# Attention softmax denominators: reciprocals by GpSimd's power instruction, and all sums of exps made on VectorE

## The chip, the cores and the metric

One core of a Trainium2 chip. The metric is device microseconds of the whole kernel, the median of several executions. The engines are called as in the profile: PE (TensorE matmuls, PEld its weight loads), DVE (VectorE), ACT (ScalarE), POOL (GpSimd), SP (SyncE; all DMA issues on the page of before are its queue's, SPq).

## The reference, cut to what matters

A transformer block on 2048 tokens of width 1024: modulated layer norm, attention with 32 query heads of 32 that share one key and value head, output projection, then a second layer norm and a gated MLP of width 3584. The change touches one line of it, the softmax:

```python
scores = jnp.einsum('bhqd,bkd->bhqk', q, k) * Dh ** (-0.5)
p = _softmax(scores, axis=-1)
o = jnp.einsum('bhqk,bkd->bhqd', p, v)
```

## The kernel before

The kernel works on query blocks of 256, 256, 512, 512 and 512 tokens. Within a block it runs eight rounds, one for each group of four heads. In a round, PE makes scores (L704), ACT makes exps of them (L715) into a ring of ten buffers U, PE multiplies the exps by the values (L659) and adds the result to the numerators ASB, and the denominators of the four heads come to DSB. At the end of a round the product ASB/DSB is written over the queries in QT. While a block is in its rounds, PE fills its free time with the MLP of the block before. What is left runs after the last round, together with the last block's MLP; this is called the tail below.

The instructions are put in a fixed order by a list scheduler in the kernel's own code. It uses the durations that are written at each `G.add` as `dur`. Each engine gets its instructions in this fixed order.

The denominators come in one of two ways. For the first `NDIR` = 2 rounds of a block (0 in the first block), PE multiplies every exp tile by ones ("direct"). For the others DVE adds four exp tiles at a time (L744, L749) into a buffer TR, and PE multiplies these few sums by ones (L760):

```python
elif w == 1:
    G.add("dve", lambda e, tr=tr, u=u, fu=first_u: e.tensor_tensor(        # L744
        TR[:, tr, 0:4 * W], U[:, fu, 0:4 * W], U[:, u, 0:4 * W], ALU.add), ...)
else:
    G.add("dve", lambda e, tr=tr, u=u: e.tensor_tensor(                     # L749
        TR[:, tr, 0:4 * W], TR[:, tr, 0:4 * W], U[:, u, 0:4 * W], ALU.add), ...)
# ... (cut: dmm, the matmul by ones over the sums, into the PSUM bank of group g)
G.add("dve", lambda e, g=g: e.tensor_copy(DSB[:, 0:qn], PB[g.bank][:, 0:qn]), writes=["DSB"], ...)   # L766
for h in range(qn // 128):
    G.add("dve", lambda e, h=h: e.reciprocal(DSB[:, h * 128:(h + 1) * 128], DSB[:, h * 128:(h + 1) * 128]),
          reads=["DSB"], writes=[("DSBr", h), "DSB%d" % h], dur=0.87, ...)                            # L769
G.add("dve", lambda e, f=f: e.tensor_tensor(QT[:, f, q0:q0 + qn], ASB[:, 0:qn], DSB[:, 0:qn], ALU.mult),
      ..., writes=qkeys(f, q0, qn) + ["ATTD"], ...)                                                   # L771
```

There is one ASB and one DSB, and the matmuls by the values read the key "ATTD" that the product writes. So the first values batch of a round waits for the product of the round before, and an exp can only run ten buffers ahead of the values batches that free them.

The softmax here doesn't subtract the row's maximum and nothing guards it: scores larger than these inputs give would overflow.

## Time and profile before

| | before |
|---|---|
| time, median of the first 3 runs | 1299.66 us |
| profiled span | 1296.0 us |
| attention rounds, from 47 to 1097 us | 1050 us |
| tail, from 1097 us | 199 us |
| one steady round of 512 queries | 34.47 us |
| denominator's copy to product in such a round | 11.06 us |

The engine summary and the chain of waits, from the page of before. In the first line a figure is busy us, its share of the span in brackets and the number of instructions; in the others it is the share of the span that the chain spends on an engine or line:

```profile
PE 1177.5 (91%) x11393; PEld 583.5 (45%) x11393; DVE 877.7 (68%) x1223; ACT 1011.0 (78%) x1174; POOL 20.8 (2%) x51
...
PE 43%; ACT 41%; issue 6%; DVE 6%; DMA 3%; SPq 1%; ACTq 0%; DVEq 0%
```

Busy time by stretch in before: the length, then busy us and instructions of each engine, PE's clock and the DMA share.

```profile
47.00:1097.00 1050.00, 958.85 (x9773) 442.85 (x9766) 769.70 (x1022) 982.03 (x1131) 9.55 (x24) 0.97 0.34 95
1097.00:1296.00 199.00, 193.35 (x1285) 124.00 (x1283) 71.47 (x118) 16.72 (x28) 3.17 (x8) 1.00 0.47 132
```

The third busy figure is DVE's. In the rounds ACT is busy for 982 and PE for 959 of 1050 us, DVE for 770. So DVE, whose work the change moves, has the most room of the three.

Groups of instructions of before, from the page: line, engine, operation, output and input, count, then busy us and mean ns of one, then idle time of the engine just before them and what ended most of it:

```profile
L715 ACT ACTIVATE UREG<-SP 128x1024 bf16<-128x1024 f32 x1024 | 969.6, 1172 | 60.6 <-PE PB L659 32.1
...
L749 DVE TENSOR_TENSOR UREG<-UREG 128x2048 bf16<-128x2048 bf16 x200 | 243.2, 1216 | 31.8 <-ACT UREG L715 29.2
...
L744 DVE TENSOR_TENSOR UREG<-UREG 128x2048 bf16<-128x2048 bf16 x100 | 121.5, 1215 | 87.3 <-ACT UREG L715 86.7
...
L769 DVE RECIPROCAL DSB<-DSB 128x128 f32<-128x128 f32 x128 | 115.1, 927 | 0.5
```

And the only powers of before, the layer norms' inverse roots, from the POOL groups by shape:

```profile
L474 POOL TENSOR_TENSOR RS<-RS,NHALF 128x1 f32<-128x1 f32 x16 | 9.1, 571 | 1.3
L474 POOL TENSOR_TENSOR RS<-RS,NHALF 128x4 f32<-128x4 f32 x4 | 4.2, 1043 | 0.3
```

Finally the end of a steady round on DVE, from the timeline of before (start us, us, instruction), from the denominator's copy to the product 11.06 us later:

```profile
703.74 0.68 DVE L766 COPY DSB<-PB 128x512 f32<-128x512 f32 x1
...
714.80 0.68 DVE L771 TENSOR_TENSOR QT<-ASB,DSB 128x512 bf16<-128x512 f32 x1
```

### The profile page before, as it was taken

Reading aid. Unit: us, or ns where it says so; the run is one execution under the profiler, and the core shown is the slowest. Engines: PE = TensorE matmul, PEld = TensorE weight load, DVE = VectorE, ACT = ScalarE, POOL = GpSimd, SP = SyncE. Lnnn points to the kernel's source line nnn. Section 1 sums busy time; section 2 is a strip of 40 time slices with the busy share of each in tenths; the row PEclk is TensorE's granted clock in tenths of the full one; section 3 lists DMA queues with packets and bytes.
Section 4 is the critical chain, followed back from the end, with each engine's and each line's share of the span. In section 5 each row is a group of like instructions: output and inputs, shape, how many; then the busy total and the mean of one; then the engine's idle time right before and its main releaser. Section 6 shows DMA issues by size and latency. Waiting matters only on the chain.

```text
span 1296.0 us, 26693 instructions
## 1 busy us (share of the span) xinstructions
PE 1177.5 (91%) x11393; PEld 583.5 (45%) x11393; DVE 877.7 (68%) x1223; ACT 1011.0 (78%) x1174; POOL 20.8 (2%) x51
## 2 busy tenths in 40 slices
PE   5698998899898889868999999999999999999998
PEld 3343344554455555413333335545333336754477
DVE  7888867885457787746687777656887777633421
ACT  1499999999899999989999999989999996011100
POOL 1000000000000000000000000000000000000000
PEclk9898999999899999868999999999999999999999
DMA  9533001553456556500232344202433244255563
GB/s 313 195 103 112 2 2 50 148 155 107 114 133 176 144 151 181 145 1 2 66 89 84 90 121 112 62 1 67 130 98 94 83 109 115 60 174 150 161 173 90
DMA packets 239446, 141.31 MB, mean 109 GB/s; under 512 B 6880, under 2 KB 231136, under 8 KB 239328
## 3 DMA queue, kind: packets, MB, share of 16 engines
q1 hardware_dynamic: 239328, 139.61, 37.6%
q8 instruction: 90, 1.47, 0.5%
q14 instruction: 28, 0.23, 0.1%
HBM read 135.40 MB, written 4.19 MB: 108 GB/s over the span
## 4 chain that ended last, share of the span: by engine, by line
PE 43%; ACT 41%; issue 6%; DVE 6%; DMA 3%; SPq 1%; ACTq 0%; DVEq 0%
ACT UREG L715 38%; PE PB L809 9%; PE PB L838 7%; PE SP L704 5%; PE SP L809 5%; PE PB L659 5%; PE SP L838 5%; ACT HREG L818 3%; PE PB L786 2%; DMA WREG<-in_B_w_dram 1%; DVE UREG L744 1%; PE PB L554 1%; PE PB L760 1%; DMA WREG<-in_w_mod_dram 1%; DMA UREG<-in_w_mod_dram 1%
## 5 line engine op out<-in xcount | busy, mean ns | idle before, releaser
L715 ACT ACTIVATE UREG<-SP 128x1024 bf16<-128x1024 f32 x1024 | 969.6, 1172 | 60.6 <-PE PB L659 32.1
L809 PE MATMUL PB<-QT,WREG 128*128 128x512 bf16 (+1 forms) x1904 | 361.7, 331 | 6.8 <-DVE DSB L766 2.0
L749 DVE TENSOR_TENSOR UREG<-UREG 128x2048 bf16<-128x2048 bf16 x200 | 243.2, 1216 | 31.8 <-ACT UREG L715 29.2
L704 PE MATMUL SP<-QT,KT 32*128 32x512 bf16 (+1 forms) x2560 | 207.5, 348 | 57.8 <-ACT UREG L715 44.2
L809 PEld LDWEIGHTS PB<-QT,WREG 128*128 128x128 bf16 x1904 | 166.8, 98 | 160.7 <-issue 63.3
L744 DVE TENSOR_TENSOR UREG<-UREG 128x2048 bf16<-128x2048 bf16 x100 | 121.5, 1215 | 87.3 <-ACT UREG L715 86.7
L704 PEld LDWEIGHTS SP<-QT,KT 32*128 32x128 bf16 x2560 | 54.1, 92 | 245.4 <-ACT UREG L715 231.0
L838 PE MATMUL PB<-WREG,HREG 128*128 128x256 bf16 x1232 | 152.8, 273 | 2.7 <-DVE HREG L843 1.8
L659 PE MATMUL PB<-UREG,V 128*32 128x512 bf16 (+1 forms) x2528 | 138.1, 353 | 10.2 <-DVE HREG L820 4.6
L838 PEld LDWEIGHTS PB<-WREG,HREG 128*128 128x128 bf16 x1232 | 113.1, 98 | 40.3 <-issue 24.8
L818 ACT ACTIVATE HREG<-PB 128x512 bf16<-128x512 f32 (+1 forms) x126 | 82.2, 652 | 46.9 <-PE PB L809 42.7
L769 DVE RECIPROCAL DSB<-DSB 128x128 f32<-128x128 f32 x128 | 115.1, 927 | 0.5
L820 DVE SCALAR_TENSOR_TENSOR HREG<-HREG,PB 128x512 bf16<-128x512 bf16 (+1 forms) x126 | 71.0, 563 | 45.8 <-ACT HREG L818 37.7
L659 PEld LDWEIGHTS PB<-UREG,V 128*32 128x32 bf16 x2528 | 59.2, 99 | 69.9 <-issue 25.8
L818 ACT ACTIVATE HREG<-SP 128x512 bf16<-128x512 f32 x14 | 8.4, 597 | 94.5 <-PE SP L809 94.5
L809 PE MATMUL SP<-QT,WREG 128*128 128x512 bf16 x336 | 75.0, 379 | 0.0
L554 PE MATMUL PB<-HREG,WREG 128*128 128x512 bf16 x256 | 66.2, 384 | 1.2 <-DVE QT L557 1.1
L825 DVE TENSOR_TENSOR HREG<-HREG,PB 128x256 bf16<-128x256 bf16 (+1 forms) x112 | 60.8, 543 | 5.4 <-PE PB L809 3.9
L838 PE MATMUL SP<-WREG,HREG 128*128 128x256 bf16 x560 | 62.8, 273 | 1.3 <-DMA WREG<-in_B_w_dram 1.3
L838 PEld LDWEIGHTS SP<-WREG,HREG 128*128 128x128 bf16 x560 | 54.6, 98 | 8.8 <-DMA WREG<-in_B_w_dram 1.8
L786 PE MATMUL PB<-WO,QT 128*128 128x512 bf16 x208 | 54.7, 390 | 0.1
L809 PEld LDWEIGHTS SP<-QT,WREG 128*128 128x128 bf16 x336 | 32.9, 98 | 39.4
(88 smaller groups left out, 567.0 us busy)
## 6 DMA issues: line engine op xcount, KB each, us to landing
WREG<-in_B_w_dram SPq DMA_DIRECT2D x140, 512.0 KB, 4.1
WREG<-in_B_w_dram SPq DMA_DIRECT2D x20, 1792.0 KB, 8.2
X<-in_A_x_dram SPq DMA_DIRECT2D x32, 256.0 KB, 3.7
WREG<-in_w_mod_dram SPq DMA_DIRECT2D x16, 512.0 KB, 4.9
UREG<-in_w_mod_dram SPq DMA_DIRECT2D x8, 512.0 KB, 9.1
out_dram<-X SPq DMA_DIRECT2D x16, 256.0 KB, 3.4
WO<-in_A_wo_dram SPq DMA_DIRECT2D x1, 2048.0 KB, 16.0
WREG<-in_A_wq_dram SPq DMA_DIRECT2D x1, 1792.0 KB, 11.1
```

The source lines that it names most:

```text
L554: g = mm_group(NC, lambda e, b, c: e.matmul(b, WQ[:, c, f * P:(f + 1) * P], HT[:, c, sl], start=c == 0, stop=c == NC - 1), lambda c: [("WQ ...
L659: r = e.matmul(PB[g.bank][32 * gg:32 * gg + 32, 0:qn], V[:, kt, :] if kind == "V" else ONES[:], U[:, pu, (gg * npk + j) * qn:(gg * npk + j ...
L704: r = e.matmul(SP[:, b, o:o + w], KT[32 * gg:32 * gg + 32, kts[j] * P:(kts[j] + 1) * P], QT[32 * gg:32 * gg + 32, f, q0 + qo:q0 + qo + w], ...
L715: G.add("act", lambda e, u=u, h0=h0, n=n, b0=b0, nb=nb, wb=wb: e.activation(U[:, u, h0 * W:(h0 + n) * W].rearrange("p (b w) -> p b w", b=n ...
L744: G.add("dve", lambda e, tr=tr, u=u, fu=first_u: e.tensor_tensor(TR[:, tr, 0:4 * W], U[:, fu, 0:4 * W], U[:, u, 0:4 * W], ALU.add), reads= ...
L749: G.add("dve", lambda e, tr=tr, u=u: e.tensor_tensor(TR[:, tr, 0:4 * W], TR[:, tr, 0:4 * W], U[:, u, 0:4 * W], ALU.add), reads=[("TR", tr) ...
L769: G.add("dve", lambda e, h=h: e.reciprocal(DSB[:, h * 128:(h + 1) * 128], DSB[:, h * 128:(h + 1) * 128]), reads=["DSB"], writes=[("DSBr", ...
L786: g = mm_group(NC, lambda e, b, f, t=t, h=h: e.matmul(b, QT[:, f, t * P:(t + 1) * P], WO[:, f, h * 512:(h + 1) * 512], start=f == 0, stop= ...
L809: return e.matmul(b[:, o:o + qn], W13[sl][w][:, c, sub * P:(sub + 1) * P], QT[:, c, q0:q0 + qn], start=c == 0, stop=c == NC - 1)
L818: G.add("act", lambda e, g=g1: e.activation(TS[:, 0:qn], PB[g.bank][:, 0:qn], ACT.Tanh, scale=0.5), writes=["TS"] + alias("TS"), groups=[( ...
L820: G.add("dve", lambda e, g=g1: e.scalar_tensor_tensor(TT[:, 0:qn], TS[:, 0:qn], 1.0, PB[g.bank][:, 0:qn], ALU.add, ALU.mult), reads=["TS"] ...
L838: return e.matmul(b[:, j * 256:(j + 1) * 256], HHT[:, fc, (i0 + j) * P:(i0 + j + 1) * P], W2S[:, r, fc, :], start=fc == 0, stop=fc == NF - 1)
```

## The change

The intent: the 128 reciprocals cost DVE 115 us, and GpSimd is busy for 20.8 of 1296 us. Let GpSimd compute 1/x as x to the power of -1, in one instruction per round. DVE, relieved, can then take over the sums of the rounds that PE summed directly, which saves PE matmuls. The code plans 1.0 + 0.016 us a column for the power, 9.2 us at 512 columns.

```diff
-    NDIR = 2
+    NDIR = 0
@@
+    MONE = sb("MONE", [P, 1], F32)
@@
+    G.add("pool", lambda e: e.memset(MONE[:], -1.0), writes=["MONE"], dur=0.1)
@@
-            for h in range(qn // 128):
-                G.add("dve", lambda e, h=h: e.reciprocal(DSB[:, h * 128:(h + 1) * 128], DSB[:, h * 128:(h + 1) * 128]),
-                      reads=["DSB"], writes=[("DSBr", h), "DSB%d" % h], dur=0.87, prio=2 if f == NC - 1 else 4)
+            G.add("pool", lambda e: e.tensor_tensor(DSB[:, 0:qn], DSB[:, 0:qn], MONE[:].broadcast_to([P, qn]), ALU.pow),
+                  reads=["DSB", "MONE"], writes=["DSB"], dur=1.0 + qn * 0.016)
             G.add("dve", lambda e, f=f: e.tensor_tensor(QT[:, f, q0:q0 + qn], ASB[:, 0:qn], DSB[:, 0:qn], ALU.mult),
-                  reads=["ASB", "DSB"] + [("DSBr", h) for h in range(qn // 128)], writes=qkeys(f, q0, qn) + ["ATTD"],
+                  reads=["ASB", "DSB"], writes=qkeys(f, q0, qn) + ["ATTD"],
```

## The prediction

> **What bounds it now (1296.0 us profiled).** The chain of waits gives ACT 41% (exps alone 38%) and PE 43%. Busy time by stretch: from 47 to 1097 us (attention of five query blocks, the previous block's MLP mixed in) ACT is busy 93% (982 of 1050 us) and PE 91%; from 1097 us PE runs almost alone. In a steady round of one head group (34.5 us, 512 queries) exps and tanhs fill ACT except about 2 us. PE work that attention cannot absorb spills into the tail (1097 to 1145 us is left-over W2 and output projection). DVE is busy 68%, GpSimd 2%.
>
> **What the change removes and adds** (groups of instructions):
> - DVE: 128 reciprocals go, 115.1 us. Eight rounds that summed denominators on PE now need 6x12+2x6 = 84 more adds at 1.216 us, +102 us; their evictions fall by about 5 us. Net about -18 us, off the bound.
> - PE: 512 ones-matmuls over exps go (27.5 us), 128 over sums come (about 8 us): -20 us, in a stage where PE is 91% busy. That alone is worth perhaps 10 to 18 us.
> - GpSimd: 40 power instructions, 24 of 512 columns and 16 of 256. The old ones took 571 ns for 1 column and 1043 ns for 4[...]. The code itself assumes 1.0+0.016 us a column: 9.2 and 5.1 us, 302 us in all, hideable: from the denominator's copy to the final product a steady round took 10 to 11 us already, and the next values batch waits for that product.
>
> **The step that decides.** [...] After the change every power has adds queued right behind the denominator's copy. [...]
>
> **Prediction: 1410 us**, range 1275 to 1650. Weights: power about 9 us and blocking, 55% (1350 to 1500); about 9 us without blocking, 22% (about 1283, 1% faster); power much longer than the code assumes, 23%: at 157 ns a column (81 us) the rounds become GpSimd-bound, near 3000 us, above my range. Faster by over 2%: 0.06; within 2%: 0.17; slower by over 2%: 0.77.
>
> **What would show each step.**
> - GpSimd group: the power's mean at 512 and 256 columns (9 and 5 us, or 81 and 41).
> - The two add groups: mean stays 1.22 us if nothing blocks. If blocked, some adds last 5 to 9 us, or DVE shows as long idle that ends when the power ends. DVE groups: reciprocal gone, adds 300 to 384.
> - Waits: ACT's exps waiting for PE rise from 60 us to 150 to 250 us, in one gap per round just after the denominator's copy; PE gets waits on DVE evictions.
> - PE: ones-matmuls over exps 512 to 0, over sums 496 to 624.
> - Rounds of 34.5 us become about 39 to 40.
>
> **What would make it wrong.** [...] the power is much longer (then GpSimd-bound, as a wait of the final product on the power)[...].

In this text, passages are cut that told hardware behaviour which no trace had shown. Under "The step that decides" and "What would make it wrong" they held the author's assumption that DVE stands still while a power runs, and PE and ACT after it ("blocking"). It was not shown: in the trace of before no power overlaps an add of the sums. The sum with the cut term was 5 us lost in each of 24 rounds and 2 us in each of 16, about 150 us, less 15 us gained: 1296 + 135 = 1431 us for the branch of 55%. The record does not say how 1410 us was weighed from it and the other branches. The slope, (1043 - 571) / 3 = 157 ns, stands.

## The result, and the profile after

| | before | after |
|---|---|---|
| time, median | 1299.85 us (4 runs) | 3659.35 us (4 runs) |
| ratio, 95% interval | 1 | 2.8165 [2.8116, 2.8213] |

Here and below, a ratio is the mean time of one kernel's fast runs over that of the other's of the same rounds, so it is not quite the ratio of the medians. The change makes the kernel 2.8 times as slow. The result is correct.

The engine summary and the chain of waits, from the page of after:

```profile
PE 1229.0 (34%) x11009; PEld 590.3 (16%) x11009; DVE 874.5 (24%) x1171; ACT 1017.2 (28%) x1174; POOL 2673.9 (73%) x92
...
POOL 71%; PE 13%; ACT 8%; DVE 4%; issue 3%; DMA 1%; SPq 0%; DVEq 0%; ACTq 0%
```

POOL, 2% busy before, is 73% busy and makes 71% of the chain. No other engine has much more to do than before: PE, the largest difference, is busy 51 us longer, with fewer matmuls but at a mean granted clock of 0.667 where before had 0.975. The groups of after, from the page:

```profile
L770 POOL TENSOR_TENSOR DSB<-DSB,MONE 128x512 f32<-128x512 f32 (+1 forms) x40 | 2647.3, 66181 | 684.0 <-DVE DSB L768 684.0
L717 ACT ACTIVATE UREG<-SP 128x1024 bf16<-128x1024 f32 x1024 | 972.9, 1117 | 2203.4 <-PE PB L661 1349.4
...
L772 DVE TENSOR_TENSOR QT<-ASB,DSB 128x512 bf16<-128x512 f32 (+1 forms) x40 | 23.4, 585 | 2229.0 <-POOL DSB L770 2229.0
...
L751 DVE TENSOR_TENSOR UREG<-UREG 128x2048 bf16<-128x2048 bf16 x256 | 316.1, 1235 | 53.3 <-ACT UREG L717 49.8
...
L746 DVE TENSOR_TENSOR UREG<-UREG 128x2048 bf16<-128x2048 bf16 x128 | 156.6, 1223 | 90.0 <-ACT UREG L717 89.7
```

The page's first line mixes two widths. The POOL groups of after by shape part them:

```profile
L770 POOL TENSOR_TENSOR DSB<-DSB,MONE 128x512 f32<-128x512 f32 x24 | 1983.8, 82657 | 501.0 <-DVE DSB L768 501.0
L770 POOL TENSOR_TENSOR DSB<-DSB,MONE 128x256 f32<-128x256 f32 x16 | 663.5, 41467 | 183.0 <-DVE DSB L768 183.0
```

A power of 512 columns takes 82.7 us, not 9.2. The wait of the product for the power sums to 2229 us. The exps in turn wait 1349 us for values batches (L661, L659 of before), which wait for the product. The adds, which the prediction expected to stand still, keep their mean: 1235 and 1223 ns against 1216 and 1215.

The same end of a round as shown for before, from the DVE timeline of after:

```profile
2097.08 0.68 DVE L768 COPY DSB<-PB 128x512 f32<-128x512 f32 x1
2097.68 1.22 DVE L751 TENSOR_TENSOR UREG<-UREG 128x2048 bf16<-128x2048 bf16 x1
...
2103.33 1.22 DVE L751 TENSOR_TENSOR UREG<-UREG 128x2048 bf16<-128x2048 bf16 x1
...
2180.70 0.69 DVE L772 TENSOR_TENSOR QT<-ASB,DSB 128x512 bf16<-128x512 f32 x1 [73.23 <-POOL DSB L770]
```

The bracket is DVE's idle time before the instruction and what ended it. DVE works normally for 10 us under the running power, then runs dry: by ACT's timeline the last exp ends at 2109.7 us, and the next one waits 73.4 us for a values batch (L661), because the exps have filled the ring. From the copy to the product it is 83.6 us where it was 11.1. From one power's start to the next one's (2097.84 to 2204.89 us) it is 107.05 us, against a round of 34.47 us before. The power is 82.83 of it, and the other 24 us are the rest of the chain that can't start before the product: values batches, the remaining exps, the sums, the copy.

The whole span adds up from POOL's timeline. The first power starts at 69.2 us; 16 rounds of 256 queries take 858 us, 24 of 512 queries 2536 us, and from the last product at 3463.3 us the tail takes 194 us: 3657 us.

### The profile page after: what moved, and what is told of

It reads as the page before. It is cut to its first block, busy times and chain, and to the rows that moved or that the text cites. A ratio compares the mean times of both kernels' runs of the same rounds, so it can differ in the third digit from the quotient of the medians.

```text
span 3657.0 us, 25988 instructions
## 1 busy us (share of the span) xinstructions
PE 1229.0 (34%) x11009; PEld 590.3 (16%) x11009; DVE 874.5 (24%) x1171; ACT 1017.2 (28%) x1174; POOL 2673.9 (73%) x92
## 4 chain that ended last, share of the span: by engine, by line
POOL 71%; PE 13%; ACT 8%; DVE 4%; issue 3%; DMA 1%; SPq 0%; DVEq 0%; ACTq 0%
POOL DSB L770 71%; ACT UREG L717 7%; PE PB L661 3%; PE PB L810 2%; PE SP L810 2%; PE SP L839 2%; PE SP L706 1%; DVE UREG L746 1%; PE PB L839 1%; DVE UREG L751 1%; DVE DSB L768 1%; ACT HREG L819 1%; PE PB L556 1%; PE PB L787 0%; DVE HREG L821 0%
## 5 line engine op out<-in xcount | busy, mean ns | idle before, releaser
L770 POOL TENSOR_TENSOR DSB<-DSB,MONE 128x512 f32<-128x512 f32 (+1 forms) x40 | 2647.3, 66181 | 684.0 <-DVE DSB L768 684.0
L661 PE MATMUL PB<-UREG,V 128*32 128x512 bf16 (+1 forms) x2528 | 179.5, 435 | 1592.2 <-DVE QT L772 651.1
L772 DVE TENSOR_TENSOR QT<-ASB,DSB 128x512 bf16<-128x512 f32 (+1 forms) x40 | 23.4, 585 | 2229.0 <-POOL DSB L770 2229.0
L810 PE MATMUL PB<-QT,WREG 128*128 128x512 bf16 (+1 forms) x1904 | 373.2, 337 | 444.3 <-DVE HREG L821 295.1
L661 PEld LDWEIGHTS PB<-UREG,V 128*32 128x32 bf16 x2528 | 69.8, 117 | 1679.8 <-DVE QT L772 654.8
L751 DVE TENSOR_TENSOR UREG<-UREG 128x2048 bf16<-128x2048 bf16 x256 | 316.1, 1235 | 53.3 <-ACT UREG L717 49.8
L706 PE MATMUL SP<-QT,KT 32*128 32x512 bf16 (+1 forms) x2560 | 216.3, 363 | 53.4 <-ACT UREG L717 40.1
L746 DVE TENSOR_TENSOR UREG<-UREG 128x2048 bf16<-128x2048 bf16 x128 | 156.6, 1223 | 90.0 <-ACT UREG L717 89.7
L819 ACT ACTIVATE HREG<-PB 128x512 bf16<-128x512 f32 (+1 forms) x119 | 71.6, 601 | 165.5 <-DVE HREG L821 144.7
L474 POOL TENSOR_SCALAR RS<-MV 128x1 f32<-128x1 f32 (+1 forms) x20 | 7.9, 395 | 119.9 <-DVE MV L469 119.9
L826 DVE TENSOR_TENSOR HREG<-HREG,PB 128x512 bf16<-128x512 bf16 (+1 forms) x119 | 66.5, 559 | 14.0 <-PE PB L810 11.9
```

Of the source, the lines that this page charges most:

```text
L661: r = e.matmul(PB[g.bank][32 * gg:32 * gg + 32, 0:qn], V[:, kt, :] if kind == "V" else ONES[:], U[:, pu, (gg * npk + j) * qn:(gg * npk + j ...
L706: r = e.matmul(SP[:, b, o:o + w], KT[32 * gg:32 * gg + 32, kts[j] * P:(kts[j] + 1) * P], QT[32 * gg:32 * gg + 32, f, q0 + qo:q0 + qo + w], ...
L751: G.add("dve", lambda e, tr=tr, u=u: e.tensor_tensor(TR[:, tr, 0:4 * W], TR[:, tr, 0:4 * W], U[:, u, 0:4 * W], ALU.add), reads=[("TR", tr) ...
L770: G.add("pool", lambda e: e.tensor_tensor(DSB[:, 0:qn], DSB[:, 0:qn], MONE[:].broadcast_to([P, qn]), ALU.pow), reads=["DSB", "MONE"], writ ...
L810: return e.matmul(b[:, o:o + qn], W13[sl][w][:, c, sub * P:(sub + 1) * P], QT[:, c, q0:q0 + qn], start=c == 0, stop=c == NC - 1)
L819: G.add("act", lambda e, g=g1: e.activation(TS[:, 0:qn], PB[g.bank][:, 0:qn], ACT.Tanh, scale=0.5), writes=["TS"] + alias("TS"), groups=[( ...
```

## The experiments

Theory A is that the power's own duration, about 0.41 us plus 0.16 us a column, lies on the chain denominator, power, product, next values batch, and is the whole loss. The rivals: B, the repeated exponent makes this power slow; C, a power and DVE's adds hold each other up; D, the 84 added adds matter; E, the fixed order, planned for 9 us, is to blame; F to H below. Kernels of one group shared a chip and its runs of before (medians 1298.8 to 1299.5 us).

### The power by itself: micro_power

A separate small kernel with zeros as output: powers of several widths on an otherwise idle core, then one with the exponent as a full tile, one on 32 partitions, one in bf16, plain multiplies, and last a power and a multiply beside a row of adds like those of the sums.

```python
for n in (1, 2, 4, 8, 16, 32, 64, 128, 256, 512):
    e.tensor_tensor(RPOW[:, 0:n], DEN[:, 0:n], M1[:].broadcast_to([P, n]), ALU.pow)      # L37
e.tensor_tensor(RPOW[:], DEN[:], MT[:], ALU.pow)                 # L38, full exponent tile
e.tensor_tensor(RPOW[0:32, :], DEN[0:32, :], MT[0:32, :], ALU.pow)                       # L39
e.tensor_tensor(RB[:], DENB[:], DENB[:], ALU.pow)                # L40, bf16
# ... then beside 80 and 20 adds of 128x2048 bf16 on VectorE (L66):
e.tensor_tensor(RPOW[:], DEN[:], MT[:], ALU.pow)                 # L45
e.tensor_tensor(GC[:], GA[:], GB[:], ALU.mult)                   # L46, 2048 columns
```

> A measurement by itself, whose output is wrong on purpose (zeros). Theory A[...]: 0.41 us plus 0.157 to 0.160 us a column at every size, so about 10.6 us at 64, 41 at 256 and 82 at 512 columns; the same with a full exponent tile in place of the repeated one and the same for 32 partitions as for 128; 512 columns of multiply far cheaper, 1 to 2 us. Rival B (the repeated exponent operand is what is slow): with a full exponent tile 512 columns fall to about 9 us. Rival C[...]: with 80 exp-sum-like adds of 128x2048 bf16 beside one power, one add or the power takes about 82 us longer; without the exclusion every add stays near 1.22 us and the power near 82 us.

POOL groups by shape of micro_power:

```profile
L45 POOL TENSOR_TENSOR RPOW<-DEN,MT 128x512 f32<-128x512 f32 x1 | 83.1, 83102 | 14.0 <-DVE UC L66 14.0
L38 POOL TENSOR_TENSOR RPOW<-DEN,MT 128x512 f32<-128x512 f32 x1 | 82.1, 82137 | 0.1
L39 POOL TENSOR_TENSOR RPOW<-DEN,MT 32x512 f32<-32x512 f32 x1 | 82.1, 82127 | 0.1
L37 POOL TENSOR_TENSOR RPOW<-DEN,M 128x512 f32<-128x512 f32 x1 | 81.9, 81915 | 0.1
L40 POOL TENSOR_TENSOR RB<-DENB 128x512 bf16<-128x512 bf16 x1 | 81.9, 81915 | 0.1
...
L37 POOL TENSOR_TENSOR RPOW<-DEN,M 128x64 f32<-128x64 f32 x1 | 10.5, 10518 | 0.1
L46 POOL TENSOR_TENSOR GC<-GA,GB 128x2048 f32<-128x2048 f32 x1 | 5.5, 5467 | 18.6 <-DVE UC L66 18.6
...
L42 POOL TENSOR_TENSOR RPOW<-NUM,DEN 128x512 f32<-128x512 f32 x1 | 1.3, 1260 | 0.1
```

From 64 to 512 columns the power takes (81.92 - 10.52) / 448 = 0.159 us for each, and at 512 columns it takes 81.9 to 82.1 us on the idle core, with a repeated or a full exponent, on 32 or 128 partitions, in f32 or bf16. B falls. Here each power starts 0.1 us after the one before ends, so start to start gives the same time. Using 32 partitions in place of 128 saved nothing (82.1 us for both); using fewer columns did (10.5 us for 64). Each denominator is held in 32 partitions, so a round's 2048 different ones would fit in 16 columns, and a power of 16 columns took 2.89 us in this run. The moves between partitions that this needs were not tried. A multiply of the same tile takes 1.26 us, a 65th of it, and one of 128 columns 453 ns, so 2.1 ns a column.

For C, two adds from the DVE timeline of micro_power, taken from two short windows: the longest beside the power, then the longest beside the multiply of 2048 columns. An add alone takes 1.226 us:

```profile
446.24 2.17 DVE L66 TENSOR_TENSOR UC<-UA,UB 128x2048 bf16<-128x2048 bf16 x1
...
547.98 5.40 DVE L66 TENSOR_TENSOR UC<-UA,UB 128x2048 bf16<-128x2048 bf16 x1
```

Beside a multiply of 5.47 us, which ends at 552.30 us, the one add that starts under it takes 5.40 us, 4.17 us longer than alone, and ends at 553.38 us. So an add was held up here. Of the 66 adds that ran beside a power of 83 us one lost 0.94 us, and all the others ran at their usual rate. For the power, C falls.

### The two halves apart: sums_only and power_only

```diff
 sums_only (from before)          power_only (from after)
-    NDIR = 2                    -    NDIR = 0
+    NDIR = 0                    +    NDIR = 2
```

> Half of the change: all denominators from sums on VectorE, reciprocals as before. Theory A (the loss is the power's duration alone): within 2 per cent of before, 1285 to 1325 us, since PE saves about 20 us of matmul and VectorE gains about 97 us of adds in a stage where it is 68 per cent busy. Rival D (the 84 added adds carry a sizeable part of the loss): over 1400 us.

> The other half: reciprocals by the power on GpSimd, two head groups of each later block still summed on PE. Theory A: about as slow as the full change, 3600 to 3700 us, 40 powers of 41 and 82 us on the chain. Rival D (the sums matter): clearly below 3500 us.

sums_only took 1297.61 us, ratio 0.9987 [0.9971, 1.0004]: the same. power_only took 3661.68 us, as slow as the full change. D falls: the power alone is the loss. sums_only also shows that saving PE 18 to 20 us of matmuls (an estimate from the groups of before) bought nothing. The span went from 1296.0 to 1295.5 us. PE's busy time fell from 1177.5 to 1149.8 us by the page, but this trace lacks 89 of 11,009 matmul records, so the true fall is smaller; no_reciprocal below, with the same number of matmuls and none missing, has 1165.5.

### Is the order to blame: true_duration

```diff
-                  reads=["DSB", "MONE"], writes=["DSB"], dur=1.0 + qn * 0.016)
+                  reads=["DSB", "MONE"], writes=["DSB"], dur=0.4 + qn * 0.161)
```

> The full change with the duration that the static order assumes for the power set to what the trace shows (0.4 us plus 0.161 us a column in place of 1.0 plus 0.016). Theory A1 (the power sits in a data chain: denominator, power, product, next values batch, so the order can't hide it): within 5 per cent of 3659 us, 3480 to 3700. Rival E (the loss comes from an order planned for 9 us, which puts instructions that wait for the power in front of others that could run): near GpSimd's own busy time plus start and tail, 2900 to 3050 us.

It took 3439.17 us. That is 220 us less than after, a little below what I expected of A1, and far from the 2900 to 3050 us of E. Here an order that knows the real duration shortens the rest of the chain. POOL groups by shape of true_duration:

```profile
L770 POOL TENSOR_TENSOR DSB<-DSB,MONE 128x512 f32<-128x512 f32 x24 | 1986.2, 82757 | 460.3 <-DVE DSB L768 460.3
L770 POOL TENSOR_TENSOR DSB<-DSB,MONE 128x256 f32<-128x256 f32 x16 | 657.9, 41118 | 46.2 <-DVE DSB L768 46.2
```

POOL's idle time before a power falls from some 24 to some 20 us in steady rounds of 512 queries. In the two small blocks it falls from some 11 to 1 us a round, and by the times of their products these blocks bring 155 of the 220 us. So the order is to blame for about a tenth of the loss, and E falls as the main cause: a better order can't take the power off the chain.

### Take the chain apart: two_buffers

Two ASB and two DSB tiles, used in turn, and values batches that don't read "ATTD" any more. The order again knows the true duration, as in true_duration, so that run is the one to compare with. One TR buffer was given up for the new tiles (`NTR` 5 to 4).

```diff
-    ASB = sb("ASB", [P, 512], F32)
-    DSB = sb("DSB", [P, 512], F32)
+    ASB2 = [sb("ASB%d" % i, [P, 512], F32) for i in range(2)]
+    DSB2 = [sb("DSB%d" % i, [P, 512], F32) for i in range(2)]
@@  (batch)
-        ... for kt in pk}) + ["ATTD", "ONES"] +
+        ... for kt in pk}) + ["ONES"] +
@@  (attention; the keys "ASB" and "DSB" become ka and kd throughout)
+            ASB, DSB = ASB2[f % 2], DSB2[f % 2]
+            ka, kd = "ASB%d" % (f % 2), "DSB%d" % (f % 2)
```

> The full change with the true duration in the static order, two copies of the numerator and denominator tiles, and values batches that no longer wait for the previous product (one exp-sum buffer fewer, to make room). Theory A1 (about 20 us per round are the serial rest of the chain around each power): the powers run back to back, so about 2650 us of powers plus 69 us before the first plus 193 us after the last, 2850 to 3050 us; GpSimd over 85 per cent busy. Rival (the chain is not what spaces the powers): stays above 3300 us.

It took 3046.32 us. POOL groups by shape of two_buffers:

```profile
L772 POOL TENSOR_TENSOR DSB<-DSB,MONE 128x512 f32<-128x512 f32 x24 | 1967.5, 81996 | 0.0
L772 POOL TENSOR_TENSOR DSB<-DSB,MONE 128x256 f32<-128x256 f32 x16 | 658.1, 41159 | 25.9 <-DVE DSB L770 25.9
```

The idle time of POOL before the powers was 460.3 and 46.2 us in true_duration (501.0 and 183.0 in after); here it is 0.0 and 25.9. The powers run back to back, the steady products on DVE follow each other at 81.9 us, and until the last product the kernel is bound by POOL (87% busy over the whole span). So after's time is the powers' sum plus the serial rest of the chain, as A says. The time is at the top of what was expected, because the tail after the last product (2719.3 us) takes 325 us in place of 194.

### Less of the power: split_half and split_eighth

The power on the first half, or eighth, of the columns, and DVE's reciprocal on the others, with true durations in the order:

```diff
-            G.add("pool", lambda e: e.tensor_tensor(DSB[:, 0:qn], DSB[:, 0:qn], MONE[:].broadcast_to([P, qn]), ALU.pow), ...)
+            w0 = qn // 2                                   # split_eighth: qn // 8
+            G.add("pool", lambda e, w0=w0: e.tensor_tensor(DSB[:, 0:w0], DSB[:, 0:w0], MONE[:].broadcast_to([P, w0]), ALU.pow), ...)
+            cuts = [(a, min(a + 128, qn)) for a in range(w0, qn, 128)]
+            for a, z in cuts:
+                G.add("dve", lambda e, a=a, z=z: e.reciprocal(DSB[:, a:z], DSB[:, a:z]), ...)
```

> The change with the power on half of the columns and VectorE's reciprocal on the other half. Theory A1 (power on the round's chain): a round costs its power (41.3 us at 256 columns, 20.7 at 128) plus about 20 us and 10 us: 24x62 + 16x31 + 262 of start and tail = 2250 us, 2100 to 2400. Rival F (a fixed loss per power, whatever its width): stays near 3600 us.

> The power on an eighth of the columns only: 64 of 512 (10.5 us) and 32 of 256 (5.4 us). Theory A1: the chain from denominator to product stays near the 10 to 11 us it had before, so the power hides: within 2 per cent of before, 1285 to 1325 us. Rival G (every column of the power is exposed, in proportion): (3659-1298)/8 added, about 1590 us.

split_half took 2129.59 us, where A1's sum gave 2250 with a range of 2100 to 2400. split_eighth took 1330.88 us, ratio 1.024 [1.0223, 1.0257]: a little slower, 6 us above the range expected. G, which made it 1590 us, falls; F falls with split_half. So loss against width isn't a line. With true durations in the order, an eighth of the columns costs 31 us, half of them 830, all of them 2140 (true_duration): a part of the power hides, and what doesn't hide is paid in every round.

In split_eighth the power took 11.4 us in a steady round, and the product came 12.22 us after the denominator's copy, where before took 11.06. The steady round grew from 34.47 to 35.12 us. The hidden part is therefore about the 11 us that before already had between copy and product. The 24 rounds at 0.65 us would make 16 us. In the traces the rounds as a whole end 50 us later than in before and the tail is 17 us shorter; the first and last rounds of the large blocks lengthen more than the steady ones, and why was not tested.

### The plan with the duration it assumed: assumed_time

The order of the instructions on PE, DVE and ACT is that of after, one for one. Only the power is narrower, so that it lasts what the code had assumed. The result is wrong.

```diff
+    W0 = {512: 55, 256: 29}
@@
-            G.add("pool", lambda e: e.tensor_tensor(DSB[:, 0:qn], DSB[:, 0:qn], MONE[:].broadcast_to([P, qn]), ALU.pow),
+            G.add("pool", lambda e: e.tensor_tensor(DSB[:, 0:W0[qn]], DSB[:, 0:W0[qn]], MONE[:].broadcast_to([P, W0[qn]]), ALU.pow),
```

> The full change, instruction for instruction in the same order on every engine, with the power cut to 55 of 512 columns and 29 of 256, so that it lasts about the 9.2 and 5.1 us that the code assumed (most columns stay without a reciprocal: wrong result on purpose). It tests the branch of the prediction that had 55 per cent: a power of about 9 us that holds VectorE for its whole length, 1350 to 1500 us. Theory A (the power holds VectorE for about 1 us only, and a power as long as planned hides): within 1 per cent of no_reciprocal and before, 1285 to 1312 us, adds of at most about 2.2 us.

It took 1297.17 us, ratio 0.9996 [0.998, 1.0013]. POOL groups by shape of assumed_time:

```profile
L771 POOL TENSOR_TENSOR DSB<-DSB,MONE 128x55 f32<-128x55 f32 x24 | 236.2, 9843 | 474.3 <-DVE DSB L769 474.3
L771 POOL TENSOR_TENSOR DSB<-DSB,MONE 128x29 f32<-128x29 f32 x16 | 84.9, 5304 | 177.3 <-DVE DSB L769 177.3
```

So with a power of 9.8 and 5.3 us the same plan is neither slower nor faster than before. This is the closest control for after: only the power's width differs. The longest add of its sums took 1.30 us. Of the prediction's branches for a power of about 9 us, "not blocking" was the right one, and its gain of 1% wasn't there either.

### The power off the chain: power_unused

sums_only, with a power of 128 columns (64 in small blocks) on a constant after each denominator's copy, whose result nobody reads:

```diff
+            w0 = qn // 4
+            G.add("pool", lambda e: e.tensor_tensor(RT[:, 0:w0], MONE[:].broadcast_to([P, w0]),
+                                                    MONE[:].broadcast_to([P, w0]), ALU.pow),
+                  reads=["DSB", "MONE"], writes=["RT"], dur=0.4 + w0 * 0.161)
```

> sums_only, and after each denominator's copy a power of 128 columns (64 in the small blocks) on a constant, whose result nobody reads: 24x20.7 + 16x10.5 = 665 us of GpSimd off the chain. Theory A (the power costs only by being waited for): within 1.5 per cent of sums_only, 1290 to 1317 us, adds near 1.22 us, POOL about 50 per cent busy. Rival C (a running power holds VectorE up): the adds stand still for up to 20 us a round, over 1450 us.

It took 1307.78 us, ratio 1.0076 [1.0058, 1.0094] to before, about 10 us over sums_only (1297.61, another chip; both chips ran before at 1299). POOL was busy for 711 us, 686 of it these powers, and the adds kept 1218 and 1214 ns. So 686 us of power off the chain cost some 10 us, while on the chain they cost nearly all that does not hide. Most of the 10 us can be found in the trace, where a layer norm's inverse root stands behind a power in POOL's order (600.78 to 621.52 us) and DVE waits for it:

```profile
622.45 1.17 DVE L489 TENSOR_SCALAR XN<-X,MV,RS 128x1024 bf16<-128x1024 bf16 x2 [8.50 <-POOL RS L477]
```

sums_only has no such wait, and the block with this one lasts 280.8 us against 271.8 there. No run removed this wait by itself.

### What would a free reciprocal be worth: no_reciprocal

The change with the power removed, result wrong:

```diff
-            G.add("pool", lambda e: e.tensor_tensor(DSB[:, 0:qn], ..., ALU.pow),
-                  reads=["DSB", "MONE"], writes=["DSB"], dur=1.0 + qn * 0.016)
```

> The change without any reciprocal at all (the product multiplies by the denominator, so the result is wrong on purpose). It shows what a free reciprocal would be worth. Theory A (VectorE is not the bound): no faster than sums_only by more than 1 per cent, 1280 to 1300 us, although VectorE does 115 us less. Rival H (the reciprocals are on the bound): below 1250 us.

It took 1296.84 us, ratio 0.9991 [0.9974, 1.0008]: a free reciprocal is worth nothing here, and H falls. Busy time by stretch in no_reciprocal, cut where its last product starts (1058 us), as before was cut at 1097 us:

```profile
47.00:1058.00 1011.00, 911.07 (x9134) 412.81 (x9135) 749.84 (x954) 977.47 (x1125) 17.84 (x24) 0.96 0.33 92
1058.00:1295.00 237.00, 230.07 (x1531) 148.00 (x1529) 81.31 (x133) 20.30 (x34) 3.16 (x8) 1.00 0.50 138
```

The rounds did become 39 us shorter, and the tail became 38 us longer. PE did 911 us of work in the rounds, 48 less than before, and 230 in the tail, 37 more. The faster attention only pushed MLP work out of its gaps into the tail, where PE does it nearly alone. So, with all sums on DVE and the order that this scheduler makes, no cheaper reciprocal can be expected to pay; the same test with `NDIR` 2 was not run.

### The same intent with another reciprocal: newton and its controls

newton uses seven GpSimd instructions, 1.26 us for each of five and 0.62 us for each of two at 512 columns in micro_power: a first guess by an integer subtraction of the denominator's bits from a constant, then two Newton steps. It adds two scratch tiles, and `NTR` is 4 in place of 5.

```diff
-            G.add("pool", lambda e: e.tensor_tensor(DSB[:, 0:qn], ..., ALU.pow), ...)
+            G.add("pool", ... e.tensor_tensor(RX.bitcast(I32), MAG.broadcast_to([P, qn]), DSB.bitcast(I32), ALU.subtract), ...)
+            for _ in range(2):
+                G.add("pool", ... e.tensor_tensor(RT, DSB, RX, ALU.mult), ...)
+                G.add("pool", ... e.tensor_scalar(RT, RT, -1.0, 2.0, ALU.mult, ALU.add), ...)
+                G.add("pool", ... e.tensor_tensor(RX, RX, RT, ALU.mult), ...)
```

> The change's intent with another reciprocal on GpSimd: a first guess by an integer subtraction from a magic constant and two Newton steps of multiply, scale-and-add, multiply: from the single measurements 5 x 1.26 + 2 x 0.62 = 7.5 us at 512 columns, one exp-sum buffer fewer to make room. Theory A (duration alone decides): within 2 per cent of before, 1280 to 1310 us. Rival C (GpSimd and VectorE exclude each other, which the single measurement showed for multiplies but hardly for the power): the adds of each round stand still for up to 7.5 us, seen as adds of 1.5 to 2.5 us, and if the stall reaches PE and ACT as my prediction had it, 1350 to 1450 us.

It is correct and took 1363.03 us, ratio 1.049 [1.0474, 1.0506], although its instructions, as measured alone, sum to 5 x 1.26 + 2 x 0.62 = 7.5 us. Three controls followed. sums_fewer_buffers is sums_only with `NTR` 4. multiplies_unused adds to that the seven instructions on constant tiles with no reader, and leaves the orders of DVE, PE and ACT as they were but for one moved instruction on DVE and four places on PE. newton_planned is newton with longer durations in the order:

```diff
 newton_planned
-            tt, ts = 0.2 + qn * 0.00207, 0.22 + qn * 0.00078
+            tt, ts = 0.2 + qn * 0.0032, 0.27 + qn * 0.0022
```

> sums_only with one exp-sum buffer fewer (4 for 5), the control for newton and multiplies_unused, which had to make room. Expected within 1 per cent of sums_only, 1290 to 1310 us. Rival: if the buffer matters, 1330 us or more, and newton's loss is the buffer's and not the multiplies'.

> sums_fewer_buffers, and after each denominator's copy the seven GpSimd instructions of newton on constant tiles, whose result nobody reads; the orders of PE, VectorE and ACT are the same as in sums_fewer_buffers but for a few instructions. Theory C (newton lost to the mutual exclusion of VectorE's two-input adds and GpSimd's multiplies): adds of up to 2.3 us again, GpSimd's multiplies stretched from 1.26 to about 1.9 us, and 15 to 60 us over the control. Rival A (newton lost because its result came late, 14.0 us after the denominator's copy where before took 11.1): within 0.7 per cent of the control.

> newton with the durations that the static order assumes set to what they were beside VectorE's adds (about 1.84 us a multiply and 1.4 us a scale-and-add at 512 columns, in place of 1.26 and 0.62). If what newton lost beyond multiplies_unused (1363 against 1318 us) came from its result arriving later than planned, most of that comes back: 1315 to 1335 us. If it came from something else, it stays within 1 per cent of 1363 us.

| kernel | median us | ratio to before |
|---|---|---|
| sums_only | 1297.61 | 0.9987 |
| sums_fewer_buffers | 1306.65 | 1.0061 |
| multiplies_unused | 1317.87 | 1.0149 |
| newton | 1363.03 | 1.049 |
| newton_planned | 1370.00 | 1.055 |

One buffer less costs some 9 us. The same multiplies, unread, cost 11 us more. The two kernels ran on the same chip in nearly the same orders; the adds are busy 28 us longer in multiplies_unused (means of 1272 and 1309 against 1210 and 1214 ns), GpSimd's multiplies of 512 columns take 1.50 us where they took 1.26 alone, and the layer norms wait for POOL no longer than in the control (7.7 us in both), so that the two engines hold each other up is the cause that is left. This is less than the 15 to 60 us I expected of C. The adds of the sums, DVE groups by shape, first in sums_fewer_buffers and then in newton:

```profile
L749 DVE TENSOR_TENSOR UREG<-UREG 128x2048 bf16<-128x2048 bf16 x256 | 309.9, 1210 | 36.9 <-ACT UREG L715 34.8
L744 DVE TENSOR_TENSOR UREG<-UREG 128x2048 bf16<-128x2048 bf16 x128 | 155.4, 1214 | 37.7 <-ACT UREG L715 37.2
```

```profile
L754 DVE TENSOR_TENSOR UREG<-UREG 128x2048 bf16<-128x2048 bf16 x256 | 366.6, 1432 | 45.3 <-ACT UREG L720 42.9
L749 DVE TENSOR_TENSOR UREG<-UREG 128x2048 bf16<-128x2048 bf16 x128 | 163.7, 1279 | 51.0 <-ACT UREG L720 50.7
```

In newton the adds are busy 65 us longer in all (366.6 + 163.7 against 309.9 + 155.4), and GpSimd's multiplies are stretched as well, from 1.26 to 2.01 and 1.67 us. Its product comes 14.03 us after the denominator's copy in a steady round, against 11.95 in sums_fewer_buffers and 11.06 in before. The remaining 45 us of newton over multiplies_unused stay unexplained in their split: telling the order about the longer durations did not bring them back (1370 us), so "later than planned" is not the answer. Whether it is the longer standstill of DVE or the later product was not told apart.

No kernel beat before by a margin clear of noise.

## Why the prediction was right or wrong, point by point

- **The power's duration: wrong, and this is the step that failed.** The prediction says: "The code itself assumes 1.0+0.016 us a column: 9.2 and 5.1 us", 302 us in all, "hideable", and gives 77% to a power of about 9 us. It measured 82.7 and 41.5 us in the kernel, 2647 us in all, and did not hide: the product waited 2229 us for it. The prediction had the right number before it, "157 ns a column", from two lines of the profile of before, and took a planning constant in the code for better evidence than the trace. Multiplied out, the trace's line gives 0.41 + 512 x 0.157 = 81 us. The branch "near 3000 us" got 23% and lay outside the stated range. That a slowdown was forecast at all rested for the most part (55%) on the blocking, which did not happen; the direction was right by luck there.
- **The size in that branch: low.** The prediction's "the rounds become GpSimd-bound, near 3000 us" counted the powers and too little of the serial rest of the chain. The powers are 2647 us; POOL's 684 us of idle before them are mostly the chain's rest, of which the right duration in the order took away 178 us (true_duration, 3439 us) and the second buffers nearly all of the remainder (two_buffers, 3046 us).
- **The step called decisive, that DVE stands still for the whole power: wrong.** An add lost 0.94 us beside an 83 us power (micro_power), and the adds' mean in after is 1.22 to 1.24 us. With the power at its assumed duration the same plan takes 1297 us (assumed_time), not the 1350 to 1500 us of that branch. A standstill was measured beside a multiply: 5.40 us for an add beside one of 5.47 us, where an add alone takes 1.226 us. In the kernel the unread multiplies went with 11 us (multiplies_unused against sums_fewer_buffers).
- **VectorE's balance: right in its terms, too large in its sum.** 300 adds became 384, the reciprocals went, and DVE's busy time in a run without a slow power (assumed_time) is 873 us against 878, 4 less where I had estimated 18 less.
- **PE's saving of 20 us, "worth perhaps 10 to 18 us": wrong.** sums_only and no_reciprocal show the span unmoved, although PE's busy time fell: by 12 us in no_reciprocal, and by at most 28 in sums_only, whose trace lacks some matmuls. no_reciprocal shows the give-back for a faster attention: 39 us gained in the rounds, 38 lost in the tail. For the matmuls saved in sums_only, the rounds end 6 us later (last product at 1103 us in place of 1097) and the tail is 6 us shorter.
- **The chain of waits: right in shape.** The prediction named "a wait of the final product on the power" for a long power; it is 2229 us. It also named that "the next values batch waits for that product"; it is the exps' wait of 1349 us.

## What to carry to other kernels

Cost a moved instruction with the slope between two shapes of it in the trace, not with a duration written in the code, and multiply it out to the new shape before anything else: a power of 1.04 us on 4 columns was one of 82.7 us on 512. Then ask whether the freed engine bounds anything, by removing the work altogether with a wrong result: here a free reciprocal was worth nothing. Last, ask whether the result of an otherwise idle engine arrives within the time that the chain already allows: here 10.8 us from copy to product cost nothing (assumed_time), and 12.2 us went with a loss of 31 us (split_eighth).
